# Attention's score matmuls in 128x64 tile pairs, in a kernel of attention, routed experts and a dense network

## The chip, the cores and the metric

The kernel runs on one core of a Trainium2 chip. The metric is the device time of one execution in microseconds (us), the median over runs. Engines are named as in the profile: PE is TensorE's matmuls, PEld its weight loads, DVE is VectorE, ACT is ScalarE, POOL is GpSimd, SP is SyncE.

## The reference

Attention of 4 batches with 8 heads each. The 1152 queries of a head are averaged in pairs to 576; keys and values have 1152 rows of 64. The result is read as 2304 tokens of 512, goes through one of 8 experts, chosen per token, and then through a dense network.

```python
q_pool = q.reshape(B, H, S // 2, 2, D).mean(axis=3)
scores = scale * np.matmul(q_pool, k.transpose(0, 1, 3, 2))
scores = scores - np.max(scores, axis=-1, keepdims=True)
attn = np.exp(scores)
attn = attn / (np.sum(attn, axis=-1, keepdims=True) + 1e-09)
attn_out = np.matmul(attn, v)
# tokens x: e = argmax of (x @ w_gate + modality_bias); gate = its softmax
out[mask] = gate_w[mask, None] * (np.maximum(x[mask] @ w1[e], 0.0) @ w2[e])
# dense: (softplus(out @ w_in)) @ w_out
```

## The kernel before

Two heads of 64 dimensions share the 128 partitions, which gives 16 head pairs `p`. A head pair has its queries in two halves of 288 (`HQ`) and its keys in nine chunks of 128, so attention is a loop over 288 steps `g`, 18 to a head pair, 9 to a half.

Before a head pair's scores can be exponentiated, the maximum of each row is needed. `srow` works on rows of it: nine query tiles (`TILES`) times three stretches of 384 keys (`KW`), 27 rows to a head pair. For the eight tiles with h<2 one f16 matmul (L117) gives 128 queries by 384 keys into a PSUM bank `sr` (three buffers); for the tile (2,0), which holds the first 64 queries of both heads, two matmuls (L120) write 64 partitions each. DVE reduces the bank to a maximum (L121). `mfin` turns the nine maxima into f16 parts and puts them, by small matmuls (L140, L144), as two extra rows into the second plane of `Q`.

`smat(g)` computes the scores of a step transposed, 128 keys by 288 queries for each of the two heads, into `st` (two buffers): a matmul with `KA` (L168) and one with `KB` (L169) that adds the low part and the negative row maximum. `ex(g)` exponentiates both heads at once on ACT into `P` (five buffers, L172). `add(g)` sums the exponentials on POOL (L186), in head pair 14 on DVE; `rsum` adds them over partitions by matmuls with 32 columns of weights (L197, L202). `pv(g)` multiplies by the values: per step two matmuls (L212), one for each head, with 64 columns of weights each, that write partitions 0 to 63 and 64 to 127 of the bank `pv`. They are issued for two steps together at each odd chunk, and for the last chunk alone: five bursts in nine steps, 160 in all.

The order on every engine is written out by hand (`manual_schedule`): a step `g` issues `smat(g+1)`, `ex(g+1)`, then the events due at this step (`ev`: casts and loads of later head pairs, `rsum`, the routing steps of `lstage`, conversions of dense weights) between rows, then `pv`, further rows, then `add(g)`. How many rows a step has is set by `rows(g)`. The routing steps use transposes with 96 columns of weights (L238, L285) and small matmuls of 96 columns (L296 to L298), all of the 128x128 tile shape.

A weight tile of up to 32 columns is a 128x32 tile of PE's array, one of up to 64 columns a 128x64 tile, a wider one takes 128x128. The profile prints the rows and columns of a weight tile as 128*64 and so on. After attention come the experts (L608 to L610) and the dense network (L779 to L781), which the change does not touch.

Of the kernel before, what the change touches and what calls it, by code (L numbers as in the profile page):

```python
# [16 lines left out]
def attention(ctx,late,tc,I,C,x_dram,LG,gate,fill,early):  # L17

    nc=tc.nc
# [89 lines left out]
    def srow(r):  # L109
        p,w=divmod(r,SRN); t,kh=divmod(w,3)  # L110
        ka,q=KA[p%NS],Q[p%NS]
        if w==0: MX[p]=smp.tile([128,9,3],F32,name="mx")
        sr=srp.tile([128,512],F32,name="sr")
        h,r0=TILES[t]
        k0=kh*KW
        if h<2:
            nc.tensor.matmul(sr[:,:KW],lhsT=q[:,h,0,r0:r0+128],rhs=ka[:,h,k0:k0+KW],start=True,stop=True)  # L117
        else:
            for hh in range(2):
                nc.tensor.matmul(sr[64*hh:64*hh+64,:KW],lhsT=q[:,hh,0,r0:r0+64],rhs=ka[:,hh,k0:k0+KW],start=True,stop=True)  # L120
        nc.vector.tensor_reduce(out=MX[p][:,t,kh:kh+1],in_=sr[:,:KW],axis=AX.X,op=ALU.max,negate=True)  # L121

    def mfin(p,ta=0,tb=9):
# [36 lines left out]
    def dec(g):  # L160
        p,s=divmod(g,18); half,c=divmod(s,9)
        return p,half,c
    def smat(g):
        p,half,c=dec(g); ka,kb,q=KA[p%NS],KB[p%NS],Q[p%NS]
        st=stp.tile([128,2,512],F32,name="st"); ST[g]=st
        qs=slice(half*HQ,half*HQ+HQ); ks=slice(c*128,c*128+128)
        for h in range(2):
            nc.tensor.matmul(st[:,h,:HQ],lhsT=ka[:,h,ks],rhs=q[:,h,0,qs],start=True,stop=False)  # L168
            nc.tensor.matmul(st[:,h,:HQ],lhsT=kb[:,h,ks],rhs=q[:,h,1,qs],start=False,stop=True)  # L169
    def ex(g):  # L170
        P[g]=pp.tile([128,2,HQ],F32,name="P")
        nc.scalar.activation(out=P[g],in_=ST.pop(g)[:,:,:HQ],func=ACTF.Exp,scale=1.0/16)  # L172
# [235 lines left out]
    while done<6: srow(done); done+=1  # L408
    C['cl1'](); C['setup']()
    while done<15: srow(done); done+=1  # L410
# [4 lines left out]
    while done<R0: srow(done); done+=1  # L415
    for f in MF[1:]: f()
    smat(0); ex(0)
    ones()
    for g,f in C['later']: at(g,f)
# [7 lines left out]
    for g in range(NG+1):  # L427
        if g+1<NG: smat(g+1)
        if g>=1 and g-1<NG:
            p,half,c=dec(g-1)  # L430
            if c==NCH-1: evac(p,half)
        if g+1<NG: ex(g+1)
        tgt=rows(g)
        es=ev.pop(g,[])
        while pend and pend[0][0]<=g: pend.pop(0)[1]()
        while done<tgt-(g<18) or es:
            if done<tgt-(g<18): row(g)
            if es: es.pop(0)()

        if g<NG:  # L440
            c=dec(g)[2]
            for k in ((g-1,g) if c%2 else (g,) if c==NCH-1 else ()): pv(k)
        while done<tgt: row(g)
        if g<NG: add(g)
# [599 lines left out]
```

## Time and profile before

| | us |
|---|---|
| median of 3 runs (1170.28 to 1175.97) | 1172.93 |
| the profiled execution | 1169.95 |
| its span, first to last instruction | 1168.1 |
| PE busy (7887 matmuls) | 1120.9 |
| DVE busy | 865.9 |
| ACT busy | 641.3 |
| POOL busy | 468.5 |

Starts count from the first instruction. Busy times are unions over a stretch; the ends of matmuls are modelled, so distances between starts tell more of PE than its busy time. A wait is written as "who waits <- who released it"; "issue" is idle time that no semaphore in the profile explains.

### The profile page before, as it was taken

What the parts mean: (1) busy time and instruction counts of PE and PEld (TensorE: products, weight loads), DVE (VectorE), ACT (ScalarE), POOL (GpSimd) and SP (SyncE); (2) the same over time, 40 slices, a digit from 0 to 9 for tenths busy, and PEclk for the clock granted to TensorE, in tenths of its full rate; (3) what the DMA queues carried; (4) which work ended last, traced back from release to release, by engine and by line L of the source; (5) the groups of instructions that cost most, each with busy time, mean ns of one, the idle gap of its engine ahead of it and who ended that gap; (6) DMA issues with size and microseconds to landing.
All of it is one profiled execution on the core that took longest, in us unless ns stands there. A gap on an engine that the chain in (4) does not pass through costs nothing. (4 is left out here: it accounts for less than half of the span.)

```text
span 1168.1 us, 20814 instructions
## 1 busy us (share of the span) xinstructions
PE 1120.9 (96%) x7887; PEld 829.3 (71%) x7887; DVE 865.9 (74%) x1583; ACT 641.3 (55%) x1096; POOL 468.5 (40%) x512
## 2 busy tenths in 40 slices
PE   5899999999999999999999999999999999999996
PEld 2444555455545555579999999998888888889995
DVE  5778798769876888689798878659667666766662
ACT  5666656766667655647555666555444444444440
POOL 6888877898788866722221121100000100100100
PEclk9999999999999999999999999999999999999998
DMA  9334436341743151436778887531000000000000
GB/s 240 83 83 108 118 89 179 99 118 59 193 115 109 35 145 39 164 94 217 238 249 281 284 272 272 187 90 43 19 1 27 36 5 14 37 5 6 37 10 30
DMA packets 42939, 129.47 MB, mean 111 GB/s; under 512 B 5841, under 2 KB 12881, under 8 KB 40914
## 3 DMA queue, kind: packets, MB, share of 16 engines
q1 hardware_dynamic: 39794, 118.12, 33.9%
q0 software_dynamic: 3040, 9.96, 2.5%
q8 instruction: 65, 1.06, 0.4%
q14 instruction: 40, 0.33, 0.1%
HBM read 108.13 MB, written 20.45 MB: 110 GB/s over the span
## 5 line engine op out<-in xcount | busy, mean ns | idle before, releaser
L121 DVE TENSOR_REDUCE mx<-sr 128x1 f32<-128x384 f32 x432 | 225.4, 549 | 93.0 <-PE sr L117 74.1
L172 ACT ACTIVATE P<-st 128x576 f32<-128x576 f32 x288 | 186.1, 651 | 153.6 <-PE st L169 142.1
L186 POOL TENSOR_TENSOR acc<-P 128x288 f32<-128x288 f32 x192 | 160.2, 856 | 84.4 <-ACT P L172 80.7
L212 PE MATMUL pv<-P,v 128*64 128x288 f32 x1152 | 174.3, 419 | 0.3 <-ACT P L172 0.3
L788 POOL DMA_INDIRECT out_dram<-io,CIDS x18 | 18.7, 1039 | 383.2 <-ACT io L786 335.5
L169 PE MATMUL st<-Q,KB 128*128 128x288 f16 x576 | 153.3, 287 | 2.4 <-ACT Q L152 2.4
L168 PE MATMUL st<-Q,KA 128*128 128x288 f16 x576 | 155.2, 290 | 0.0
L186 POOL TENSOR_TENSOR acc<-acc,P 128x288 f32<-128x288 f32 x176 | 147.7, 860 | 8.5 <-ACT P L172 6.9
L117 PE MATMUL sr<-KA,Q 128*128 128x384 f16 x384 | 113.2, 334 | 17.9 <-DVE mx L121 9.1
L609 PE MATMUL l<-xf,WIH 128*128 128x256 f32 (+1 forms) x384 | 129.1, 336 | 0.1
L608 PE MATMUL l<-xf,WIH 128*128 128x256 f32 (+1 forms) x384 | 129.0, 336 | 0.0
L610 PE MATMUL l<-xf,wl 128*128 128x256 f32 (+1 forms) x384 | 129.0, 336 | 0.0
L645 ACT CAST mhl<-mraw 128x512 fp32r<-128x512 f32 x160 | 97.0, 618 | 54.7 <-PE l L610 22.2
L212 PEld LDWEIGHTS pv<-P,v 128*64 128x64 f32 x1152 | 70.3, 136 | 73.6 <-issue 35.6
L646 DVE TENSOR_TENSOR mhl<-mraw,mhl 128x512 fp32r<-128x512 f32 x140 | 96.3, 707 | 32.9 <-ACT mhl L645 32.4
L168 PEld LDWEIGHTS <-KA 128*128 128x128 f16 x576 | 56.3, 98 | 86.0 <-issue 76.0
L779 PE MATMUL o<-WOH,g 128*128 128x512 f32 x288 | 112.3, 390 | 0.0
L780 PE MATMUL o<-wl,g 128*128 128x512 f32 x288 | 112.2, 390 | 0.0
L781 PE MATMUL o<-WOH,g 128*128 128x512 f32 x288 | 112.0, 389 | 0.0
L762 ACT ACTIVATE e<-e 128x1024 f32<-128x1024 f32 x36 | 38.2, 1060 | 100.3 <-DVE m L760 100.3
L754 DVE TENSOR_SCALAR m<-l 128x512 f32<-128x512 f32 x72 | 49.4, 687 | 57.1 <-ACT e L753 57.0
L94 POOL TENSOR_TENSOR KB<-kr,KA 64x576 f16<-64x576 f32 x64 | 83.6, 1311 | 4.6 <-ACT KA L90 2.4
(260 smaller groups left out, 2543.0 us busy)
## 6 DMA issues: line engine op xcount, KB each, us to landing
mraw<-in_wm_dram SPq DMA_DIRECT2D x80, 512.0 KB, 4.6
kr<-in_k_dram SPq DMA_DIRECT2D x30, 576.0 KB, 9.5
qr<-in_q_dram SPq DMA_DIRECT2D x16, 576.0 KB, 6.5
v<-in_v_dram SPq DMA_DIRECT2D x16, 576.0 KB, 4.4
mraw<-in_w_out_dram SPq DMA_DIRECT2D x16, 512.0 KB, 4.4
stg<-in_w_in_dram SPq DMA_DIRECT2D x12, 512.0 KB, 6.2
y_dram<-w SPq DMA_DIRECT2D x20, 256.0 KB, 4.4
xs_dram<-xs SPq DMA_DIRECT2D x24, 192.0 KB, 2.1
```

The costliest lines, as they stand in the source:

```text
L117: nc.tensor.matmul(sr[:,:KW],lhsT=q[:,h,0,r0:r0+128],rhs=ka[:,h,k0:k0+KW],start=True,stop=True)
L121: nc.vector.tensor_reduce(out=MX[p][:,t,kh:kh+1],in_=sr[:,:KW],axis=AX.X,op=ALU.max,negate=True)
L168: nc.tensor.matmul(st[:,h,:HQ],lhsT=ka[:,h,ks],rhs=q[:,h,0,qs],start=True,stop=False)
L169: nc.tensor.matmul(st[:,h,:HQ],lhsT=kb[:,h,ks],rhs=q[:,h,1,qs],start=False,stop=True)
L172: nc.scalar.activation(out=P[g],in_=ST.pop(g)[:,:,:HQ],func=ACTF.Exp,scale=1.0/16)
L186: for h in range(2): nc.gpsimd.tensor_tensor(out=A[:,h],in0=B_[:,h],in1=P[g][:,h],op=ALU.add)
L212: nc.tensor.matmul(t[64*h:64*h+64,:HQ],lhsT=V[p][:,c,64*h:64*h+64],rhs=P[g][:,h],start=(c==0),stop=(c==NCH-1))
L608: nc.tensor.matmul(o,lhsT=wh_,rhs=x[0],start=first,stop=False)
L609: nc.tensor.matmul(o,lhsT=wh_,rhs=x[1],start=False,stop=False)
L610: nc.tensor.matmul(o,lhsT=wl_,rhs=x[0],start=False,stop=last)
L779: nc.tensor.matmul(o,lhsT=g[:,0,i,cs],rhs=WOH[:,fc],start=(fc==0),stop=False)
L780: nc.tensor.matmul(o,lhsT=g[:,0,i,cs],rhs=WOL(fc),start=False,stop=False)
```

## The change

`srow` issues the row-max scores of every tile as two matmuls with 64 columns of weights each, which write partitions 0 to 63 and 64 to 127 of the same bank; for the tile (2,0) nothing changes. `smat` does the same with the 128 keys of a chunk: each of its four matmuls becomes two with 64 keys each, on the same 288 queries. What is computed, the buffers and the order of the work stay the same.

```diff
-        if h<2:
-            nc.tensor.matmul(sr[:,:KW],lhsT=q[:,h,0,r0:r0+128],rhs=ka[:,h,k0:k0+KW],start=True,stop=True)
-        else:
-            for hh in range(2):
-                nc.tensor.matmul(sr[64*hh:64*hh+64,:KW],lhsT=q[:,hh,0,r0:r0+64],rhs=ka[:,hh,k0:k0+KW],start=True,stop=True)
+        for i in range(2):
+            hh,r=(h,r0+64*i) if h<2 else (i,r0)
+            nc.tensor.matmul(sr[64*i:64*i+64,:KW],lhsT=q[:,hh,0,r:r+64],rhs=ka[:,hh,k0:k0+KW],start=True,stop=True)
...
-        qs=slice(half*HQ,half*HQ+HQ); ks=slice(c*128,c*128+128)
+        qs=slice(half*HQ,half*HQ+HQ)
         for h in range(2):
-            nc.tensor.matmul(st[:,h,:HQ],lhsT=ka[:,h,ks],rhs=q[:,h,0,qs],start=True,stop=False)
-            nc.tensor.matmul(st[:,h,:HQ],lhsT=kb[:,h,ks],rhs=q[:,h,1,qs],start=False,stop=True)
+            for i,w in enumerate((ka,kb)):
+                for o in (0,64):
+                    nc.tensor.matmul(st[o:o+64,h,:HQ],lhsT=w[:,h,c*128+o:c*128+o+64],rhs=q[:,h,i,qs],start=(i==0),stop=(i==1))
```

## Rows read from the trace of the kernel before

**Rows 1.** The page: the span of the profiled execution.

```profile
span 1168.1 us, 20814 instructions
```

**Rows 2.** Stretches: A:B, length, busy us (x instructions) by engine, clock, DMA.

```profile
core 0: us, PE busy (x) PEld busy (x) DVE busy (x) ACT busy (x) POOL busy (x), PEclk, DMA share, GB/s
148.00:164.40 16.40, 15.41 (x132) 8.17 (x130) 16.09 (x45) 10.97 (x21) 14.10 (x16) 1.00 0.19 53
...
239.60:253.10 13.50, 13.50 (x106) 7.08 (x105) 10.84 (x22) 10.50 (x18) 12.82 (x14) 1.00 0.82 228
253.10:268.30 15.20, 15.20 (x133) 7.73 (x131) 7.95 (x19) 9.30 (x18) 12.19 (x16) 1.00 0.08 25
...
510.00:560.00 50.00, 47.08 (x442) 45.78 (x442) 46.78 (x124) 31.87 (x59) 12.66 (x11) 1.00 0.52 166
560.00:700.00 140.00, 136.95 (x1144) 135.16 (x1144) 114.78 (x189) 82.82 (x150) 28.32 (x22) 1.00 0.81 272
```

**Rows 3.** Waits from 26 to 510 us: total, times, longest.

```profile
ACT P L172 <- PE st L169: 141.0, 157, 3.0
...
DVE mx L121 <- PE sr L117: 66.8, 88, 2.1
...
PE sr L117 <- DVE mx L121: 8.4, 11, 1.4
```

**Rows 4.** Timeline of PE about one L212 burst: start, length, instruction.

```profile
303.09 0.33 PE L117 MATMUL sr<-KA,Q 128*128 128x384 f16 x1
303.34 0.46 PE L212 MATMUL pv<-P,v 128*64 128x288 f32 x2
...
303.63 0.41 PE L212 MATMUL pv<-P,v 128*64 128x288 f32 x2
303.98 0.30 PE L168 MATMUL st<-Q,KA 128*128 128x288 f16 x1
...
304.11 0.29 PE L169 MATMUL st<-Q,KB 128*128 128x288 f16 x1
304.24 0.29 PE L168 MATMUL st<-Q,KA 128*128 128x288 f16 x1
304.36 0.29 PE L169 MATMUL st<-Q,KB 128*128 128x288 f16 x1
```

**Rows 5.** Timeline of PE: L120's pair before an L212 burst, and after L169.

```profile
300.48 0.35 PE L120 MATMUL sr<-KA,Q 128*64 128x384 f16 x2
300.66 0.41 PE L212 MATMUL pv<-P,v 128*64 128x288 f32 x2
...
300.90 0.65 PE L212 MATMUL pv<-P,v 128*64 128x288 f32 x4
...
302.11 0.29 PE L169 MATMUL st<-Q,KB 128*128 128x288 f16 x1
302.32 0.35 PE L120 MATMUL sr<-KA,Q 128*64 128x384 f16 x2
```

**Rows 6.** Waits from 26 to 510 us, of PE's weight loads.

```profile
PEld L168 <- issue: 72.9, 172, 1.5
...
PEld pv L212 <- issue: 35.6, 118, 1.6
...
PEld pv L212 <- ACT P L172: 10.9, 21, 1.9
```

**Rows 7.** Weight loads: L202's beside its matmuls (timeline); durations of L120, L117 (by line).

```profile
308.52 0.43 PE L202 MATMUL sr<-acc,one 128*32 128x144 f32 x8
308.53 0.13 PEld L202 LDWEIGHTS sr<-acc,one 128*32 128x32 f32 x4
308.65 0.31 PE L202 MATMUL sr<-acc,one 128*32 128x144 f32 x4
...
L120 PEld LDWEIGHTS <-Q x96: 106/106/177, 11.1 to 450.8; 128*64 128x64 f16 x96
...
L117 PEld LDWEIGHTS <-Q x384: 95/98/147, 6.7 to 467.4; 128*128 128x128 f16 x192
```

## Prediction

> **What bounds the kernel now.** I first cut the span into stages. Up to about 510 us attention runs, with the routing inside it; then experts and a dense network follow. The diff touches attention alone. The stage rows show that in attention TensorE (PE) is busy nearly throughout, but PE's busy time is modelled, so it is not proof [rows 2]. The waits say it better: between 26 and 510 us VectorE (DVE) sits idle 66.8 us for row-max scores of L117, and ScalarE (ACT) 141.0 us for scores of L169, while the longest of PE's own waits comes to 8.4 us [rows 3]. The other engines wait for PE; PE waits for almost nothing. So in attention the time is what PE's stream of matmuls takes, and the question is what that stream is made of.
>
> The third view is a timeline of PE alone, read by the distance from one start to the next. A 288-column f16 matmul on a full 128x128 tile costs 0.12 to 0.13 us (304.11 to 304.24 to 304.36) [rows 4]. The 384-column one costs 0.16 (I take it in proportion, 0.12 x 384/288; the L120 pair below confirms it). The products of L212 come as pairs: two matmuls on 128x64 tiles start together, and a pair costs 0.24 (300.66 to 300.90) [rows 5].
>
> Now the borders. L117 (128x128) to the first L212 pair takes 0.25 instead of 0.16, and that first pair takes 0.29 (303.34 to 303.63) instead of 0.24 [rows 4]. The last L212 pair to L168 takes 0.35 instead of 0.24 [rows 4]. L169 to an L120 pair takes 0.21 instead of 0.12 [rows 5]. But L120 to L212, both on 128x64, takes 0.18, and the L212 pair after it 0.24: no border cost but 0.02, although the type goes from f16 to f32 there [rows 5]. So what costs is the change of tile shape, not the type: 0.09 + 0.05 = 0.14 us into L212, 0.09 + 0.02 = 0.11 into an f16 pair, 0.11 back out. Between 26 and 510 us the weight loads of L168 had such an idle gap ahead of them 172 times, those of L212 118 times, with nothing else to explain it ("issue") [rows 6].
>
> **The change part by part.**
>
> *The pairs themselves.* 384 row-max matmuls (8 of 9 tiles, three each, 16 head pairs) and 288 x 4 = 1152 score matmuls become pairs: 1536 pairs, as many instructions more and as many weight loads more. Row tile 2 (L120) was such a pair already. Each half has the same columns to stream as the whole had, so a pair costs what the one matmul cost if (a) the halves run side by side and (b) the weights of the next pair load beside the running one. For (a): L120's pair gives way after 0.18 with 384 columns in each half [rows 5]; one after the other they would take 0.32. For (b) the trace has no f16 pair of 288 columns following another at this speed, so I bound it. The nearest row is harder: four 128x32 tiles of L202 have eight instructions per group and weights that take 0.13 us in all beside a group of 0.13 (308.52 to 308.65) [rows 7]. One f16 half-width load took 106 ns against 98 ns for a full one [rows 7]. 106 fits under 120. Lower bound: nothing; below nothing is excluded, since the columns streamed are the same. Upper bound: a load wholly exposed, 1536 x 0.106 = 163 us. I take 0, by L202's row.
>
> On this point the Trainium skill speaks against the change: TensorEngine Tiling (Array Packing), Gotcha 2, says that column tiling rules out the fast weight load, and TensorE: Matmul & The Clock Gate, Part 3, The mechanism, that weight loads run beside matmuls only in other row groups, which a pair of 128-row tiles hasn't got. By that rule the loads would be exposed and the sum would be the 163 us above. The trace disagrees: the loads of L202 run at 308.53 while L202's matmuls run from 308.52 to 308.95, on the same 128 rows [rows 7].
>
> *The switches removed.* Stepping through PE's matmuls up to 515 us in order of start, I count 500 changes of shape; [rows 6] groups the idle gaps that most of them leave. Into L212 from a 128x128 tile there are 142, of which 127 come from L117 or L169 and go; the others follow transposes and the like of the routing steps, which stay 128x128. Back from 64 to 128 there are 179; 36 remain or arise, so 143 go. Into f16 pairs from 128 there are 37; 23 will be there, 14 fewer. The 142 switches that have a 32-column tile on one side keep their number, with 64 in place of 128 beside them. The sum: 127 x 0.14 + 143 x 0.11 + 14 x 0.11 = 17.8 + 15.7 + 1.5 = 35 us.
>
> *What the other engines take back.* I cut attention into 32 halves of nine steps and split the 35 us by the switches in each: 1.2 to 1.5 us in a plain half, 0.5 to 0.6 in a half with routing steps, where shapes still alternate. Then I ask whether DVE or GpSimd (POOL) has room. In the half from 148.0 DVE is busy 16.09 of 16.40 us, and two others are like it: their 0.6 us each are lost, 1.8 [rows 2]. In the half from 239.6 POOL is busy 12.82 of 13.50: it can give 0.4 of 1.3, and one more is like it; lost 1.8 [rows 2]. Two or three near 0.92 lose 0.5 each. That makes 5. In the half from 253.1 DVE has 7.95 of 15.20 us to do and POOL 12.19, and all of the gain stays [rows 2]. Next, 21 of the 160 bursts of L212 already wait for ACT's exponentials rather than for the switch [rows 6]; there the cheaper way in gains nothing: 21 x 0.14 = 3 us. Together 35 - 5 - 3 = 27 us.
>
> *After attention.* From 560 to 700 us PE is busy 136.95 of 140 us while DMA moves 272 GB/s at a share of 0.81 [rows 2]. Its weight loads are issued as buffers come free, so they move forward with it; between 510 and 560 DMA is half idle (0.52) and can take a stage that comes 27 us earlier [rows 2]. I cost this at nothing; if that cover is gone, a stage that is fed at 0.81 could lose a few us.
>
> The profiled execution took 1169.95 us, 1.9 outside its span of 1168.1 [rows 1]; less 27 it is 1143. The median of the three runs is 3 us above it, so 1172.93 - 27 = 1146.
>
> **The rivals.**
>
> *The other engines set the pace.* For: DVE and POOL are each busy near 0.8 of attention and have crowded halves. If every half in which either is above 0.88 keeps its length, those 17 halves hold 16 of the 35 us, and with the 3 us of late exponentials the gain is 16: 1157. Against: POOL's and DVE's own idle is mostly waiting for PE or for what PE feeds [rows 3].
>
> *Everything stays.* Three score banks and five exponential buffers smooth the crowded halves into their neighbours: 1173 - 35 = 1138.
>
> *Slower: weight loads show between pairs.* Half-width loads come twice as often, and if the array can't take the next pair's weights while both halves of it stream, each pair ends with an exposed load. The decision lies at 35/1536 = 0.023 us per pair. At the whole 0.106 it would be 163 - 35 = 128 us slower, 1301. For: no f16 pair of 288 columns stands back to back in the trace. Against: [rows 7]. This is the Trainium skill's rule of above as a mechanism of this kernel, with its time.
>
> *The change doesn't do what it says.* The border cost might belong to the way from score matmuls to products and not to the shape: 1173. Against: L169 to L120 is f16 to f16 on the same operands and pays 0.09, and L120 to L212 pays next to nothing [rows 5].
>
> **How the numbers follow.** Forecast (1141 to 1150) 0.50; other engines set the pace (1150 to 1161) 0.25; everything stays (1134 to 1141) 0.15; no effect 0.05; slower 0.05. From 1136 to 1161 leaves out no effect, slower and some of the best case, 0.15 to 0.2. About 0.5%, 6 us, is what a measurement of this kernel can tell from no change: faster by more 0.90, within it 0.05, slower 0.05.
>
> **What would show it.** In PE's timeline after, L117 to L212 should take 0.16 and the first L212 pair 0.24; L212 to the first score pair 0.24; a score pair 0.12. The weight loads of L168 and L212 should lose most of their idle ("issue"). DVE's wait for L117 should shrink well below 66.8 us, and PE's waits for DVE, ACT's for POOL, should grow. Score pairs at 0.14 or more, or border costs that stay, would make the prediction wrong; so would a stage from 560 us on that grows longer.

## The result and the profile after

The changed kernel takes 1160.68 us (median of four runs, 1158.74 to 1161.83); the kernel before, on the same chip, 1172.18. The ratio is 0.9901, 95% interval 0.9885 to 0.9918: faster by 11.5 us, where 27 were forecast. The profiled execution of after took 1161.83 us, 8.1 less than that of before.

In after the named lines have moved up by one to four: the row-max scores are L118 (their maximum on DVE is L119), the scores L168 (both pairs of one loop), the exponentials L171, the products L211, the sum on POOL L185. L86 and L94, which come up below, stand where they stood.

The page of after: its span, and the clock that PE was granted, in tenths, in 40 slices of 29 us.

```profile
span 1160.0 us, 23887 instructions
...
PEclk8989999998999999999999999999999999999999
```

and the clock row of before:

```profile
PEclk9999999999999999999999999999999999999998
```

The span is 8.1 us shorter than in [rows 1]. New in after are the eights early in the clock row.

From here on attention means the stretch from the first score matmul to the first product of the stage behind it. Its row in before and in after (columns as in [rows 2]: stretch, length, busy time and instructions by engine, granted clock as a share, DMA share, GB/s):

```profile
20.00:506.40 486.40, 466.32 (x3717) 242.96 (x3717) 379.19 (x817) 308.86 (x562) 387.82 (x439) 1.00 0.41 110
```

```profile
20.20:496.50 476.30, 444.22 (x5239) 310.70 (x5239) 386.31 (x817) 309.75 (x563) 385.94 (x439) 0.97 0.42 113
```

Attention is 10.1 us shorter, what follows 1.8 longer (663.5 us for 661.7). PE's busy time fell by 22.1 us, more than twice what attention gained, and the mean clock fell from 1.00 to 0.97.

The timeline of PE in after, around the same kind of burst as in [rows 4] and [rows 5]:

```profile
305.20 0.29 PE L168 MATMUL st<-Q,KA 128*64 128x288 f16 x2
305.33 0.29 PE L168 MATMUL st<-Q,KB 128*64 128x288 f16 x2
305.45 0.29 PE L168 MATMUL st<-Q,KA 128*64 128x288 f16 x2
305.57 0.29 PE L168 MATMUL st<-Q,KB 128*64 128x288 f16 x2
305.69 0.33 PE L118 MATMUL sr<-KA,Q 128*64 128x384 f16 x2
305.86 1.14 PE L211 MATMUL pv<-P,v 128*64 128x288 f32 x8
306.83 0.29 PE L168 MATMUL st<-Q,KA 128*64 128x288 f16 x2
```

and a weight load beside the first of these pairs:

```profile
305.20 0.11 PEld L168 LDWEIGHTS <-KB 128*64 128x64 f16 x2
```

Score pairs start 0.12 to 0.13 us apart, as single matmuls did; L118 to L211 takes 0.17, the first L211 pair 0.24 (the next one starts at 306.10), and the next score pair starts at 306.83, 0.97 after the first of four L211 pairs, so the way back takes 0.24 too. The loads for KB run while the pair of KA streams. Neither a border cost nor an exposed weight load is left here.

The waits from 26 to 510 us in after (total us, times, longest):

```profile
ACT P L171 <- PE st L168: 121.8, 152, 5.2
DVE mx L119 <- PE sr L118: 77.8, 102, 5.3
PE sr L118 <- DVE mx L119: 16.2, 19, 3.4
PEld L168 <- issue: 7.0, 26, 0.6
...
PEld pv L211 <- issue: 4.4, 22, 0.3
PEld pv L211 <- ACT P L171: 3.2, 11, 0.8
```

The idle ahead of the weight loads is gone: 72.9 us to 7.0 for the scores, 35.6 to 4.4 for the products [rows 6]. Ahead of the row-max weights it grew, from 21.8 us (L117 and L120) to 32.1, and PE's wait for DVE's maxima doubled, from 8.4 us [rows 3] to 16.2; one of these waits is 3.4 us long. The other engines still wait for PE most of the time: ACT 121.8 us for scores (141.0 before), DVE 77.8 for row-max scores (66.8, and 15.9 for L120, before).

The wait of 3.4 us is the clearest place. The timeline of POOL, DVE and PE there, first in before (start, length, instruction, idle of the engine before it):

```profile
72.75 3.02 POOL L94 TENSOR_TENSOR KB<-kr,KA 64x576 f16<-64x576 f32 x2
73.22 1.42 DVE L86 TENSOR_TENSOR Q<-qs,Q 64x576 f16<-64x576 f32 x1
75.16 0.32 PE L117 MATMUL sr<-KA,Q 128*128 128x384 f16 x1 [1.41 <-DVE mx L121]
```

and in after:

```profile
71.25 2.51 POOL L94 TENSOR_TENSOR KB<-kr,KA 64x576 f16<-64x576 f32 x2
71.72 3.40 DVE L86 TENSOR_TENSOR Q<-qs,Q 64x576 f16<-64x576 f32 x1
...
73.73 2.04 POOL L185 TENSOR_TENSOR acc<-P 128x288 f32<-128x288 f32 x2
75.05 1.94 DVE L119 TENSOR_REDUCE mx<-sr 128x1 f32<-128x384 f32 x4
75.65 0.53 PE L118 MATMUL sr<-KA,Q 128*64 128x384 f16 x2 [3.36 <-DVE mx L119]
75.92 2.18 PE L211 MATMUL pv<-P,v 128*64 128x288 f32 x8
77.84 0.50 PE L168 MATMUL st<-Q,KA 128*64 128x288 f16 x2
78.08 0.50 PE L168 MATMUL st<-Q,KB 128*64 128x288 f16 x2
```

DVE's subtraction L86 (the low part of the queries) is held while POOL runs L94 and then L185: 3.40 us, where the shortest L86 took 0.75. The maxima queue behind it, the score banks stay full, and PE waits 3.36 us. Then comes the second thing: a score pair takes 0.24 us instead of 0.12, and eight products 2.18 instead of 1.14. For 6.8 us the granted clock is the lower of its two levels, 1.2 GHz for 2.4. In attention of before the clock doesn't fall at all; in after it does at 22.3, 73.5 and 268.0 (6.8 us each) and at 387.5 (3.4 us).

How often it falls differs between executions. Over its whole span the profiled one was granted 0.986 of the full clock, the other three 0.990, 0.994 and 0.990. That is some 32, 23, 14 and 23 us at the lower level (an estimate: twice the missing share of the span); the times are 1161.83, 1161.2, 1158.74 and 1160.16 us. So the profile shows the execution of after with the most of it.

### The profile page after: what moved, and what is told of

Same layout as the page of the kernel before. It is cut to its first block, busy times and chain, and to the rows that moved or that the text cites. A ratio compares the mean times of both kernels' runs of the same rounds, so it can differ in the third digit from the quotient of the medians.

```text
span 1160.0 us, 23887 instructions
## 1 busy us (share of the span) xinstructions
PE 1100.4 (95%) x9423; PEld 899.2 (78%) x9423; DVE 873.5 (75%) x1583; ACT 641.9 (55%) x1096; POOL 467.7 (40%) x512
## 5 line engine op out<-in xcount | busy, mean ns | idle before, releaser
L119 DVE TENSOR_REDUCE mx<-sr 128x1 f32<-128x384 f32 x432 | 223.8, 549 | 82.5 <-PE sr L118 79.8
L171 ACT ACTIVATE P<-st 128x576 f32<-128x576 f32 x288 | 185.9, 650 | 134.9 <-PE st L168 122.6
L185 POOL TENSOR_TENSOR acc<-P 128x288 f32<-128x288 f32 x192 | 158.8, 848 | 79.3 <-ACT P L171 76.8
L211 PE MATMUL pv<-P,v 128*64 128x288 f32 x1152 | 173.5, 415 | 0.5 <-ACT P L171 0.5
L787 POOL DMA_INDIRECT out_dram<-io,CIDS x18 | 19.2, 1068 | 382.6 <-ACT io L785 334.9
L118 PE MATMUL sr<-KA,Q 128*64 128x384 f16 x864 | 137.6, 341 | 28.2 <-DVE mx L119 16.9
L168 PE MATMUL st<-Q,KB 128*64 128x288 f16 x1152 | 159.8, 290 | 3.0 <-ACT Q L150 3.0
L168 PE MATMUL st<-Q,KA 128*64 128x288 f16 x1152 | 160.4, 291 | 0.0
L185 POOL TENSOR_TENSOR acc<-acc,P 128x288 f32<-128x288 f32 x176 | 148.7, 865 | 5.6 <-ACT P L171 3.0
L211 PEld LDWEIGHTS pv<-P,v 128*64 128x64 f32 x1152 | 86.8, 139 | 31.4 <-issue 4.4
L118 PEld LDWEIGHTS <-Q 128*64 128x64 f16 x864 | 58.7, 112 | 54.8 <-issue 38.5
L168 PEld LDWEIGHTS <-KB 128*64 128x64 f16 x1152 | 73.6, 111 | 26.1 <-issue 4.1
```

The costliest lines, as they stand in the source:

```text
L118: nc.tensor.matmul(sr[64*i:64*i+64,:KW],lhsT=q[:,hh,0,r:r+64],rhs=ka[:,hh,k0:k0+KW],start=True,stop=True)
L168: nc.tensor.matmul(st[o:o+64,h,:HQ],lhsT=w[:,h,c*128+o:c*128+o+64],rhs=q[:,h,i,qs],start=(i==0),stop=(i==1))
L185: for h in range(2): nc.gpsimd.tensor_tensor(out=A[:,h],in0=B_[:,h],in1=P[g][:,h],op=ALU.add)
L211: nc.tensor.matmul(t[64*h:64*h+64,:HQ],lhsT=V[p][:,c,64*h:64*h+64],rhs=P[g][:,h],start=(c==0),stop=(c==NCH-1))
```

## The experiments

My theory after the result: the switches are gone at about the price summed, and two losses took the gain: POOL holds DVE, so that PE waits, and the clock falls behind PE's waits. The rival: the price of the switches was wrong, and so much was never to be had. Experiments 1 and 2 test the price, 3 to 8 take away one cause each, 9 and 10 ask for the change's worth where the other engines have room. All run beside the kernel before; a ratio is to that. "Stream" is the length of attention less PE's waits of over 150 ns there (before: 486.4 - 19.1 = 467.3 us; after: 476.3 - 31.1 = 445.2).

**1. The scores alone as pairs (e1_scores_only).** The second hunk of the change without the first: L168 is pairs, L117 stays as before.

> The scores of smat alone go in 128x64 pairs; the row-max scores of srow stay 128x128. Theory (a change of tile shape costs 0.11 to 0.14 us, a pair itself costs nothing): stepping through the order of matmuls with this one replacement gives 640 changes of shape up to 515 us instead of 500, worth 76 us instead of 60, so TensorE has 16 us more to do and the kernel is slower than before by some 10 to 18 us (1182 to 1190). Rival (the border cost belongs to the way from score matmuls to products, or pairs of scores save something by themselves): the scores stand on both sides of most product bursts, so most of the gain of the full change would be there, 1162 to 1166.

Measured: 1177.83 us, ratio 1.003 (1.0014 to 1.0046). Attention:

```profile
20.10:511.20 491.10, 480.27 (x4871) 263.40 (x4869) 378.60 (x817) 310.01 (x562) 383.64 (x439) 1.00 0.40 109
```

Half of the change is 0.3% slower than none, since scores and row-max scores now differ in shape and alternate. The stream grew by 13.8 us (481.1), near the 16 that the switches sum to; PE's waits shrank from 19.1 to 10.0, which the expectation left out, so the time stays below its 1182 to 1190.

**2. The row-max scores alone as pairs (e2_rowmax_only).** The first hunk without the second.

> The row-max scores of srow alone go in 128x64 pairs; the scores of smat stay 128x128. Theory (cost by change of shape): 702 changes instead of 500, worth 80 us instead of 60, so slower than before by some 14 to 22 us (1186 to 1194). Rival (cost not by shape): no slower than before, 1165 to 1173. With both parts apart slower and both together faster, the shape would be what counts.

Measured: 1184.15 us, ratio 1.0088 (1.0058 to 1.0117).

```profile
19.90:518.40 498.50, 485.53 (x4087) 241.28 (x4087) 379.31 (x817) 309.93 (x562) 384.25 (x439) 1.00 0.40 108
```

The stream grew by 18.7 us (486.0; summed 20), PE's waits shrank to 12.5, and the time is again a little below what was expected. So the price of a switch about stands, seen from the other side, and the rival falls. And a slower PE gets 7 to 9 us back from its waits: the waits are a term that moves with the stream, in either direction.

**3 and 4. Before and after without the low part of the queries (e3_before_no_low, e4_after_no_low).** L86, the operation that was held, is left out (30 times on DVE and twice on POOL), and its tile zeroed once. The kernels leave out this correction of the scores.

```
-                ve.tensor_tensor(out=q[t:t+64,h,0],in0=QS[p][o:o+64],in1=q[o:o+64,h,0],op=ALU.subtract)
+                pass
...
+                nc.gpsimd.memset(Q[i][o:o+64,h,0],0.0)
```

> The kernel before without the 32 subtractions that make the low part of the queries (28 of them on VectorE, 0.75 to 3.4 us each); that half of the query tile is zero instead, so this leaves out a part of the scores' precision. It is the other half of the comparison with the next run. Theory (TensorE's stream bounds the kernel before): little is gained, 2 to 7 us below the kernel before (1165 to 1170). Rival (VectorE bounds attention already): 20 us or more below.

> The changed kernel without the same subtractions, the low part of the queries zero. Theory (the 27 us were in TensorE's stream, but VectorE, held up in these subtractions while GpSimd works, keeps TensorE waiting for score banks, and in those waits the granted clock falls to half): the distance to the run without them and without the change is 22 to 30 us (about 1138 to 1145), and the clock stays full in attention but for the start. Rival 1 (pairs save TensorE only some 12 us): the distance stays 9 to 14 us. Rival 2 (GpSimd and ScalarE pace attention): it stays 9 to 16 us, with ScalarE's waits for GpSimd grown and the clock full.

Measured: before without it 1171.11 us, ratio 0.9976 (0.9964 to 0.9988); after without it 1152.4, 0.9828 (0.9797 to 0.9858). The distance is 18.7 us instead of 11.5.

```profile
18.00:504.30 486.30, 469.15 (x3716) 244.13 (x3717) 349.70 (x789) 309.77 (x564) 373.98 (x430) 0.99 0.41 111
```

```profile
18.00:484.10 466.10, 438.83 (x5240) 307.78 (x5239) 356.19 (x789) 310.08 (x564) 373.51 (x430) 1.00 0.43 116
```

Thirty microseconds less work for DVE left attention of before as long as it was (486.3 for 486.4) and took 10.2 us off that of after (466.1 for 476.3). But the clock differs in both comparisons. The profile of experiment 3 has falls that before has not (from 16.1 to 26.3, begun ahead of attention, and 3.4 us at 289.1; hence 0.99 in its row): PE waits 3.0 us less there (16.1), and its stream is 2.9 longer (470.2). What DVE's work was worth in before is therefore not shown to be nothing. Experiment 4 has one fall in attention (259.3, 3.4 us) for after's four, and its profiled execution is the fastest of its kernel (1148.41; the slowest took 1158.25 at a mean clock of 0.985), so part of its 10.2 us is clock. The distance of 18.7 us lies between the 22 to 30 that I expected and the 9 to 16 of the rivals. PE's waits in attention are still 26.2 us without L86.

**5. Only the collision at 71 us moved (e5_late_key_lows).** POOL's key lows (L94) of one head pair come six steps later, so that L86 no longer runs beside two of them in a row; same work.

```
-            put(14*p-19+3*i//4 if p<5 else ...
+            put(14*p-19+3*i//4+(6 if p==2 and 'ckl' in f.__qualname__ else 0) if p<5 else ...
```

> The changed kernel with one thing moved: GpSimd's four subtractions for the low parts of the keys of head pair 2 come six steps later, so that VectorE's subtraction for the queries of that head pair does not run beside two of them in a row. Theory (VectorE is held 3.4 us in that one subtraction while GpSimd works, TensorE waits 3.4 us for a score bank and the clock falls to half for 6.8 us): that subtraction takes at most 1.5 us, the wait goes below 1.5 us, the half clock near 73 us goes, and the nine steps from 68.6 us on take 15 to 16 us instead of 20.1; the kernel 1155 to 1158. Rival (the nine steps are long because VectorE has that much to do): they stay within 1 us of 20.1 and the kernel at 1160.

Measured: 1153.49 us, a little better than expected, ratio 0.9828 (0.9806 to 0.985). The two L86 of that place, beside which POOL runs L185 (66.38 to 71.97), take 1.19 and 0.93 us instead of 3.40 for the one:

```profile
67.35 1.19 DVE L86 TENSOR_TENSOR Q<-qs,Q 64x576 f16<-64x576 f32 x1
...
69.63 0.93 DVE L86 TENSOR_TENSOR Q<-qs,Q 64x576 f16<-64x576 f32 x1
```

Attention is 463.2 us, 13.1 less than in after, from one edit in one place. That is more than its own stall can give, and the rest was not touched: the falls of the clock at 22.3, 268.0 and 387.5 are absent too in the execution that was profiled (this kernel's four were granted 0.993 to 0.995 of the clock). The half that begins at 260.5 in after, and the same half here, with the same instructions:

```profile
260.50:298.20 37.70, 33.35 (x357) 21.29 (x355) 31.78 (x89) 20.16 (x38) 25.92 (x31) 0.91 0.36 93
```

```profile
253.10:287.10 34.00, 29.95 (x359) 19.74 (x356) 32.08 (x89) 20.19 (x38) 25.91 (x31) 1.00 0.42 103
```

They are 3.7 us apart at alike waits of PE (4.4 and 4.1 us by the sum of its gaps; ahead of the place of the fall the same 1.5 and 1.0), and PE's busy time makes 3.4 of that. So the fall costs about 3.4 us there, and PE's wait alone does not decide whether it comes. Experiment 4 says the same: it has these two waits in both routing stages, at 255.5 and 373.3, and a fall after the first alone.

**6. Filler matmuls (e6_filler).** At the places of the falls, and in the routing near 146 where there was none, PE gets pairs of matmuls into unused columns of a score bank to do while it would wait; nobody reads them.

```
+    def warm(t,n):
+        for _ in range(n):
+            for o in (0,64):
+                nc.tensor.matmul(t[o:o+64,288:512],lhsT=ident16[:,0:64],rhs=KA[0][:,0,0:224],start=True,stop=True)
...
+                if g==0 and h==0 and i==1: warm(st[:,1],26)
...
+            if half==0 and b<B-1: warm(rt_,9)
...
+        if g==28: warm(ST[g+1][:,1],24)
+        if g in (74,146,218): warm(ST[g+1][:,1],12)
```

> The changed kernel with filler matmuls of 224 columns into unused columns of score banks at the places where TensorE waits ahead of the falls of the clock (one at the start, one in step 28, and in steps 74, 146 and 218 with the rank matmuls after them); nothing reads them. Theory (it is TensorE's idling there that lets the clock fall, and the half clock costs what TensorE then does at half rate): the waits stay as long as before but are filled, the clock stays full at 22, 73, 268 and 387 us, and the kernel gains 5 to 9 us (1152 to 1156). Rival 1 (VectorE sets the pace in those stretches, so the half clock costs nothing): the clock stays up and the time stays within 2 us of 1161. Rival 2 (the filler delays the work behind it): slower by up to 8 us.

Measured: 1152.15 us, ratio 0.9817 (0.9801 to 0.9834); attention 468.0, although PE has 226 matmuls more to do. The place of the stall (L164 is the filler, L216 the products):

```profile
71.38 2.49 PE L164 MATMUL st<-KA,ident 128*64 128x224 f16 x48
...
75.10 0.35 PE L118 MATMUL sr<-KA,Q 128*64 128x384 f16 x2 [1.06 <-DVE mx L119]
75.27 1.16 PE L216 MATMUL pv<-P,v 128*64 128x288 f32 x8
```

The stall ends as late in its half as in after (7.1 us from the start), but eight products take 1.16 us and not 2.18. This separates the price of the clock from that of the stall, since the stall is as long and the clock full. The half from 68.6 in after, and here:

```profile
68.60:88.70 20.10, 15.92 (x166) 10.38 (x164) 14.91 (x23) 11.51 (x21) 15.66 (x17) 0.83 0.36 89
```

```profile
68.00:85.90 17.90, 16.01 (x214) 11.67 (x212) 14.95 (x23) 11.69 (x21) 15.76 (x17) 1.00 0.40 101
```

So 2.2 us here. The other places, in after:

```profile
20.20:39.40 19.20, 15.40 (x154) 11.83 (x154) 10.99 (x24) 11.69 (x22) 16.22 (x24) 0.82 0.65 153
379.30:415.60 36.30, 31.95 (x357) 20.70 (x355) 31.84 (x89) 20.17 (x38) 25.91 (x31) 0.95 0.31 83
```

and here:

```profile
20.50:38.80 18.30, 17.09 (x204) 14.03 (x205) 11.08 (x24) 10.84 (x21) 15.78 (x24) 1.00 0.67 164
258.50:292.50 34.00, 32.08 (x400) 21.74 (x398) 32.08 (x89) 20.19 (x38) 25.91 (x31) 1.00 0.41 102
373.60:407.60 34.00, 32.06 (x399) 21.73 (x397) 32.07 (x89) 20.18 (x38) 25.91 (x31) 1.00 0.35 89
```

That is 3.7 at 268.0 (37.7 against 34.0), 2.3 at 387.5 (36.3 against 34.0) and 0.9 at 22.3 (19.2 against 18.3): 9 us for 23.8 us at half the clock. Some of it is waiting, since 6.8 and 3.4 us at half rate can by themselves lose no more than 3.4 and 1.7. By PE's stream alone the falls cost 7.5 us (445.2 in after, 437.7 in experiment 5). In experiment 5 the half from 66.1 takes 15.8 us, so the stall itself is worth another 2.1 there.

That the filler keeps the clock up holds beyond the profiles: all eight executions of the two kernels with filler (this one and experiment 8) were granted 0.997 or 0.998 of the clock over their spans, the twelve of after and of experiments 5 and 7, without it, 0.986 to 0.995 (experiment 10, with two holds eased and no filler, 0.995 to 0.998).

**7. Routing with one operation for three (e7_single_ops).** In the routing steps four DVE results are made by one tensor_tensor each instead of three tensor_scalar, as the kernel does in its last routing stage already.

```
-            if last: V.tensor_tensor(out=T('d',[96,3,8]),in0=lg,in1=e3(z['m']),op=ALU.subtract)
+            if True: V.tensor_tensor(out=T('d',[96,3,8]),in0=lg,in1=e3(z['m']),op=ALU.subtract)
...
```

> The changed kernel with four routing steps of each but the last stage done by one VectorE instruction instead of three (the largest score's subtraction, the one-hot comparison, the gate's product, the block comparison), as the last stage already does. Each of the three could be held by GpSimd; mean 0.43 us and up to 1.3 each. Theory (in the routing halves VectorE's holds set the time): VectorE's busy time in attention falls by 10 us or more, the halves from 260 and 379 us lose 2 to 4 us each, the kernel 1152 to 1157. Rival (the chain through ScalarE and TensorE between the routing steps sets it): no more than 2 us.

Measured: 1149.53 us, ratio 0.9794 (0.9778 to 0.981); attention 462.5. That is better than expected, though DVE's busy time in attention fell by 7.3 us (to 379.03) and not by 10. By line, in the routing from 146.3 to 179.4 us of after, and from 140 to 176 us here (count, then busy us, mean ns, idle before):

```profile
L265 DVE TENSOR_SCALAR OH<-cc,f 96x8 f16<-96x8 f32 x6 | 3.0, 557 | 0.0
```

```profile
L263 DVE TENSOR_TENSOR OH<-cc,f 96x24 f16<-96x24 f32 x2 | 1.3, 640 | 0.0
```

That stretch takes 33.1 us in after and 31.2 here; two others like it gain about as much beside what the clock cost them (34.0 us in experiment 5, 32.0 here, for the one above):

```profile
146.30:179.40 33.10, 30.43 (x359) 20.24 (x357) 31.32 (x91) 19.88 (x38) 25.85 (x30) 1.00 0.39 106
```

```profile
144.60:175.80 31.20, 30.10 (x361) 20.03 (x359) 28.94 (x75) 19.89 (x38) 26.07 (x30) 1.00 0.41 113
```

In after DVE is busy 31.32 of 33.10 us: it is the bound there, and the three small operations are dear because POOL holds them (an L265 takes 0.22 us where POOL is idle). Of the falls in attention only one is left, at 74.8 (3.4 us); the two in the routing are gone, and the stall at 72 us is still there.

**8. All three (e8_all_three).** The edits of 5, 6 and 7.

> The changed kernel with all three edits: later key lows, filler, single routing instructions. Theory (the 16 us that the change fell short of my sum lie in VectorE's holds and the half clock): 1146 to 1151, attention's clock full, and the distance to the kernel before 22 to 28 us. Rival (the sum of the switches was too high): it stops at 1155 or above with the clock full and TensorE's waits short.

Measured: 1148.15 us, ratio 0.9781 (0.9765 to 0.9797); attention 463.2. This is as expected. No fall of the clock is left in attention, but attention is no shorter than in 5 or 7 alone: the gains don't add. Each of the three takes some of the same falls away, and filler costs PE's time (busy 446.18 us, against 436.53 in 5); how much each of these two does is not shown.

**9 and 10. Before and after, both eased (e9_before_eased, e10_after_eased).** Edits 5 and 7, no filler, on either kernel. What is left between the two is the change, with the two holds out of its way.

> The kernel before with two of the edits that ease VectorE: GpSimd's four subtractions of head pair 2 six steps later, and single routing instructions. The control for the next run. Theory (TensorE's stream bounds the kernel before, VectorE's holds are mostly hidden there): 2 to 7 us below the kernel before (1166 to 1171). Rival (the edits are worth as much without the change): 10 us or more below.

> The changed kernel with the same two edits. Theory (the switches removed are worth about 35 us of TensorE's stream, and what was lost of it were VectorE's holds and the half clock): 22 to 28 us below the kernel before's eased form, about 1143 to 1148. Rival (the tile pairs are worth some 12 us, and the edits help either kernel alike): 10 to 15 us below it.

Measured: before eased 1165.74 us, ratio 0.9912 (0.9877 to 0.9946); after eased 1143.73, ratio 0.9719 (0.9679 to 0.9758). The distance is 22.0 us, at the edge of the 22 to 28 expected, far from the rival's 10 to 15, and twice the 11.5 of the change as it was made. The second is the fastest kernel of this study. The control missed: before eased lies 10.1 us below the kernel before beside it (1175.86), where I expected 2 to 7 and the rival said 10 or more; the interval leaves 6 to 14, and attention in its profile is only 5.3 us shorter.

```profile
19.80:500.90 481.10, 466.50 (x3718) 242.84 (x3717) 370.05 (x761) 308.42 (x562) 386.73 (x439) 1.00 0.41 112
```

```profile
19.80:477.60 457.80, 436.00 (x5241) 305.25 (x5239) 370.69 (x761) 308.68 (x562) 388.37 (x439) 1.00 0.43 118
```

Attention differs by 23.3 us: PE's stream by 29.9 (467.4 and 437.5), less 6.6 that PE waits more (13.7 and 20.3). The same two edits are worth 5.3 us in attention of before and 18.5 in that of after, whose falls they take away; over the whole kernel, by the ratios, 10 and 21.

## Why the prediction was half right

**The price of the switches was nearly right.** Thirty-five us were summed. Between experiments 9 and 10, with hardly a fall, the stream fell by 30; set against the stream of after, 445.2 us, less the 7.5 that the half clock cost it, it fell by 30 too; and the partial changes add 13.8 and 18.7 where 16 and 20 were summed. The borders measured 0.17 and 0.24 us where the prediction wrote 0.16 and 0.24. Counted in the traces of before and after, there are 284 changes of shape fewer, as summed, so each was worth 0.105 us on average. Why 5 of the 35 us did not come is not shown.

**The waits went as said in part.** PE's for DVE doubled and ACT's for POOL grew (8.6 to 9.5 us); DVE's for row-max scores hardly shrank (82.7 to 77.8 us, L120's taken in), where I had written well below.

**The pairs cost nothing, as taken.** Score pairs start 0.12 us apart, with weight loads of about 110 ns under them. The rival of exposed loads (1301) is excluded, and with it, for this kernel, the rule that spoke for it, as I read it: the Trainium skill (TensorE: Matmul & The Clock Gate, Part 3, The mechanism) says that a weight load overlaps matmuls in flight only when the row group differs. The same section also lets a load into a background weight buffer go ahead, which I had left out. "No effect" is excluded as well.

**The step that failed is "What the other engines take back".** It put 8 us there. In terms of attention the working was -35 + 8 = -27; the trace shows -30 + 12 + 7.5, about -10, and then 1.8 more behind attention. Two things were wrong with it:

- *The holds were mis-sized: PE's waits grew by 12.0 us (19.1 to 31.1) instead of 8.* I took a crowded half to keep its length, "their 0.6 us each are lost". It can get longer: the half from 268.3, one of the two that are like that from 148.0 in [rows 2], and the one after it took 33.4 us together in before, and 34.0 in experiment 5 even at the full clock; one operation for three takes 1.9 off such a pair. And a DVE operation that ran 1.42 us beside POOL ran 3.40 once the order of arrival had moved; in before L86 already took from 0.75 to 2.45 us. DVE's busy time in attention, for the same 817 instructions, grew from 379.19 to 386.31 us. I had read busy shares, and a busy share counts the time in which an operation is held as if it were work.
- *The clock was missing: 7.5 us of PE's stream, 9 by the lengths of the halves, in the execution that was profiled.* In before the granted clock was at its upper level throughout attention, so no row of it priced a fall, and I did not ask what longer waits of PE might bring. That the fall follows waits of PE is shown by experiments 6 and 8, where PE was kept busy at the same places and the clock stayed up in every execution.

The two hang together: shorter streams give longer waits, and some of these are followed by a fall. Easing both holds (experiments 9 and 10) raised the gain from 11.5 to 22.0 us. The rest, up to the 27 forecast, is mostly the stream: 30 us for 35. The added waits that stay, 6.6 us, are less than the 8 put there, and what follows attention is 2.0 us longer (666.2 for 664.2).

**Late exponentials** were put at 3 us; the wait of L211's weight loads for them came out smaller, not larger: 10.9 us [rows 6] to 3.2. That term was wrong in sign, but small.

**After attention** 0 was taken; what follows got 1.8 us longer in after, and in after the clock falls there once (530.9, 3.4 us), in before never. That this comes of the earlier start is not shown: in experiments 1 and 2, where attention ends later than in before, what follows got 1.9 and 2.7 us longer too. Where attention ends 22 to 29 us earlier it got 4.2 to 6.0 longer in experiments 5, 7 and 10, but only 0.8 in 4 and 1.3 in 8. In the first three PE waits 2.8 to 3.7 us for one gather, and a fall stands beside it (experiment 5: total us, times, longest):

```profile
PE sr L657 <- DMA io<-xs_dram,IDX: 3.7, 1, 3.7
```

In 4 this wait is 0.7 us, in 8 it does not appear. So an earlier start can cost the stage behind attention a few us, which the prediction allowed for but for another reason (the feed at 0.81); what decides it stays open.

**The rival nearest to the truth** is "the other engines set the pace" (1157; 1160.68 lies in its 1150 to 1161). It had the mechanism, DVE and POOL beside each other, but not the way: it kept crowded halves at their length, while three of them grew by 2 to 4 us (from 16.4 or 16.5 to 20.1, 20.1 and 18.7), in part by the falls of the clock. That the time fell into its range, and just inside the forecast's outer range, is luck.

**What stays open** is when the clock falls. After and experiment 5 have the same waits of 1.5 and 1.0 us near 260 us, and only after has the fall; in experiment 4 it comes at one of two such places. No row here tells them apart. Each kernel has one profile, and the granted clock over the span shows that executions of one kernel differ (0.986 to 0.994 in after, 0.994 to 0.998 in before), so the price of the clock in a single profile is not that of the median.

## What to carry to other kernels

Where TensorE alternates between tile shapes, the change of shape has a price that a timeline of starts shows (here 0.11 to 0.14 us; 0.105 on average came back), and bringing neighbours to one shape removes it, pairs of half-width tiles costing no more than a whole one; half of such a change can be worse than none. Before counting on the gain, look for operations of the next-busiest engines that already run longer beside another engine than alone: their time is not fixed and grows when the stream before them gets shorter. And price the clock: where PE's waits will grow, put other work of PE there or remove the hold, then measure again, since the two edits that were worth 5 us in attention before the change were worth 18 after it (10 and 21 over the whole kernel).

## What the runs showed of the hardware

**The DVE operations L86 and L265, on SBUF tiles alone, are held while POOL works; L119, which reads PSUM, isn't.** Durations by line over all of after (shortest, median and longest in ns):

```profile
L86 DVE TENSOR_TENSOR Q<-qs,Q x30: 751/1067/3404, 6.7 to 426.1; 64x576 f16<-64x576 f32 x30
L265 DVE TENSOR_SCALAR OH<-cc,f x21: 215/221/1315, 151.2 to 491.3; 96x8 f16<-96x8 f32 x21
L119 DVE TENSOR_REDUCE mx<-sr x432: 485/548/559, 9.5 to 461.2; 128x1 f32<-128x384 f32 x144
```

L86 takes 0.75 us with POOL idle (3 times) and 1.25 on average with POOL at work beside it (27 times), up to 3.40; even L265, an operation of 0.22 us on small tiles, takes 0.62 on average beside POOL and up to 1.3. L119 takes 549 ns on average either way. The Trainium skill states the rule (SBUF — State Buffer, Who interferes with whom: an instruction of VectorE with two SBUF inputs contends with one of GpSimd that reads SBUF); the trace of L86 agrees. The hold lasted from 71.72 to 75.12 us across several operations of POOL, 4.5 times the length of L86 alone.

**Waits of PE can be followed by 3.4 or 6.8 us at 1.2 GHz**, in which a pair of score matmuls takes 0.24 us for 0.12. Ahead of after's falls in attention PE had waited 3.0 us (22.3), 3.4 (73.5) and 1.5 and 1.0 (268.0 and 387.5). The fall can cost more than the wait: about 3.4 us behind 2.5 us of waits at 268.0. By the lengths of the halves its price was 0.1 to 0.7 us for each us at the lower clock, the upper end with some waiting in it.
